# Order of a group's matmuls on high and low parts, and the last two of a pair moved behind the next pair's first tile

## The chip, the cores and the metric

The kernel runs on one core of one Trainium2 chip. The metric is the device time of one execution in microseconds (us): 1093.27 us as the median of three runs before the change (1089.42 to 1093.37). Rows come from one profiled execution, in which a hardware profiler recorded every instruction. The core has five engines that run their own queues and meet at semaphores: TensorE (PE, matmuls; PEld is its weight load), VectorE (DVE), ScalarE (ACT), GpSimd (POOL) and SyncE (SP). DMAs are issued here from SP's and POOL's queues.

## What is computed

Channel attention over a sequence of 6016 positions and 256 channels, and two MLPs behind it (6016 x 256, hidden width 2048). In short:

```python
s = kn.transpose(0, 2, 1) @ qn / tau        # q, k normalised over the sequence: 256 x 256 scores
a = softmax(s)
x = v @ a                                   # 6016 x 256
h = x @ moe_w_in;  y = (s * relu(h)**2 + b) @ moe_w_out
h = y @ moe2_w_in; out = (max(h, 0) + alpha * min(h, 0)) @ moe2_w_out
```

## The kernel before, in words

**High and low parts.** A matmul operand in fp32r keeps fewer bits than fp32. So each fp32 operand is split: the high part is a cast of the value (by ACT, or by DVE where the planner chooses so), the low part is the value minus its high part (always on DVE, line 714 for the activations). A product is three matmuls into one PSUM bank: high data with high weights, high data with low weights, low data with high weights (`s` = 0, 1, 2 in the code).

**Stages.** The scores and the softmax take the first 60 us or so. The attention itself is folded into the first MLP's input weights (`w1_mm`, line 624), which are made in four quarters during the first pairs. Then the two MLPs run one after the other, each over six chunks of the sequence. A chunk is two blocks of 512 positions (480 in the first and the last chunk), which are the columns of the matmuls, and goes through eight *pairs*; a pair is 256 of the 2048 hidden units. There are 96 pairs, `c` = 0 to 95, eight to a chunk: pairs 0 to 47 are the first MLP, 48 to 95 the second. Pairs whose `c` is a multiple of 8 begin a chunk.

**A pair, first layer** (`a_tile`, lines 658 to 688). Four tiles: two halves of the hidden units for each of two blocks of positions. A tile is six matmuls (lines 671, 672, 674) into the one bank `h`. ACT evacuates it with the activation (lines 682 and 686), the first two tiles into `gA[c % 2]`, of which there are two copies, the last two into slots 1 and 2 of `gB`, of which there is one.

**A pair, between the layers** (`g_ops`, lines 690 to 727). The second layer is a Strassen-Winograd product, seven products in place of eight. Its seven operands are formed from the four evacuated tiles: in the second MLP by four operations at line 705 (the leaky slope), in both by four sums and differences (lines 721, 722, 724, 725). They lie in four buffers, each with a high and a low half: `G[0]` (two operands), `G[1]` (one), `G[2]` (two), `G[3]` (two). `G[3]` is made last. The cast for the high half is at line 713 (shown as line 364 where ACT does it), the low half is line 714. Each buffer exists once.

**A pair, second layer** (`b_mms`, lines 729 to 752). 21 matmuls (line 743), three for each of the products P1 to P7, each product with a PSUM bank of its own that adds up over the eight pairs of a chunk. With the bank `h` all eight banks are taken. The products and their buffers, in the order of the list: P1, P2 on `G[0]`; P3 on `G[1]`; P5, P7 on `G[2]`; P6, P4 on `G[3]`. The weights `W["wB", p]` are split in the same way.

**After a chunk** (`results`, lines 754 to 836): the banks are copied by ACT (line 364, `cb<-P`), combined by seven additions on DVE (line 774), and in the second MLP transposed on DVE (line 824) and stored; in the first MLP they get bias and scale, are split and written to memory for the second.

**What sets the order.** All this is put into a list of operations with what they read and write (class `Plan`). TensorE's operations keep the order of the list. For ACT, DVE and the DMA issues (line `sp`, in fact POOL's and SP's queues) a planner goes through an estimated time: it takes the ready operation with the earliest due time, which comes from the place of its readers in TensorE's order, and an operation that overwrites a buffer waits for the buffer's readers. Operations with no near reader (results, preparation of the second MLP's weights) are taken where nothing more urgent is ready.

TensorE's order is written out in the loop at line 890. In turn `c` the four tiles of pair `c` are emitted, and the 21 matmuls of pair `c - 1` are spread behind them (5, 5, 5 and 6):

```python
for i, u in enumerate(users):
    u()
    upto = len(bs) * (i + 1) // len(users)
    while nb < upto:
        g, r, w, us = bs[nb]
        op("pe", us, g, r, w)
        nb += 1
```

So 45 matmuls stand between one pair's start and the next one's. `g_ops(c)` and, where a chunk ends, `results` follow. From `c` = 40 to 48 the loop also emits the loads of the second MLP's weights: `wB` (line 931) and `wA` (line 935), both issued on POOL's queue, as are the loads of `x` (line 858).

Of the kernel before, what the change touches and what calls it, by code (L numbers as in the profile page):

```python
# [43 lines left out]
def est(kind, n):  # L44
    return FIXED[kind] + n * COLUMN.get(kind, 0.00085)


class Plan:
# [7 lines left out]
    def op(self, eng, us, fn, reads=(), writes=(), due=None, late=0.0, boost=0.0, after=0.0, leave=BACKLOG[0]):  # L56
        o = dict(
            i=len(self.ops), eng=(eng,) if isinstance(eng, str) else eng, us=us, fn=fn,
            pre=set(), post=[], due=due, late=late, boost=boost, after=after, leave=leave,
            left=0, end=None,  # L60
        )
        for r in reads:
            if r in self.writer:
                o["pre"].add(self.writer[r])
        for w in writes:
            if w in self.writer:
                o["pre"].add(self.writer[w])
            o["pre"].update(self.readers.get(w, ()))
        for r in reads:
            self.readers.setdefault(r, []).append(o["i"])  # L70
        for w in writes:
            self.writer[w], self.readers[w] = o["i"], []
        o["pre"].discard(o["i"])
        self.ops.append(o)
        return o
# [103 lines left out]
def tile_channel_attention_mlp_mlp(  # L179
# [56 lines left out]
    def bank(tag, name):  # L236
        return ps.tile([P, CH], F32, tag=tag, name=name)
# [124 lines left out]
    def copy(eng, o, i):  # L362
        if eng == "act":
            nc.scalar.copy(o, i)  # L364
        else:
            nc.vector.tensor_copy(o, i)
# [41 lines left out]
    with tc.manual_schedule():  # L408
# [196 lines left out]
        op = pl.op  # L605
# [3 lines left out]
        def add_unit(n, after=0.0):  # L609
            if n >= NLATE + NRAW:  # L610
                op("sp", 0.6, lambda: load_w(n), [("R",)] if n < NEARLY else [],
                   [("raw", raw_slot(n)), ("low", raw_slot(n))], late=4.0)
            parts = units.get(n) or unit_parts(n)
            for p in parts[started.get(n, 0) :]:
                op(*p[:5], late=p[5] if len(p) > 5 else 0.0, after=after)
# [74 lines left out]
        def g_ops(c):  # L690
            ph, j, p = c // 48, c // 8 % NCHUNK, c % 8
            n = sizes[j]
            a = gA[c % 2]
            k11, k21, kt, k12, k22 = ("gA", c % 2, 0), ("gA", c % 2, 1), ("gB", 0), ("gB", 1), ("gB", 2)
            V = nc.vector
            B11, B21, T1, B12, B22 = a[:, 0, :n], a[:, 1, :n], *(gB[:, i, :n] for i in range(3))
            if ph == 0:
                op("act", est("square", 2 * n), lambda: nc.scalar.activation(
                    a[:, :, :n], a[:, :, :n], AF.Square), [], [k11, k21])
                for g, kk in ((B12, k12), (B22, k22)):  # L700
                    op("act", est("square", n), lambda g=g: nc.scalar.activation(g, g, AF.Square), [], [kk])  # L701
            else:
                for f2, g, kk in ((0, B11, k11), (1, B21, k21), (0, B12, k12), (1, B22, k22)):
                    al = al_sb[:, 2 * p + f2 : 2 * p + f2 + 1]
                    op("dve", est("stt", n), lambda g=g, al=al: V.scalar_tensor_tensor(  # L705
                        g, g, al, g, op0=ALU.mult, op1=ALU.max), [], [kk])

            def hilo(k, src, keys):
                m = len(keys)
                hi, lo = (G[k][:, y, :m, :n] if m > 1 else G[k][:, y, 0, :n] for y in (0, 1))  # L710
                kh = [("Gh", k, x) for x in range(m)]
                kl = [("Gl", k, x) for x in range(m)]
                op(either, HI(m * n), lambda e: copy(e, hi, src), keys, kh, leave=BACKLOG[ph])
                op("dve", est("tt", m * n), lambda: V.tensor_tensor(  # L714
                    lo, src, hi.bitcast(F32), ALU.subtract), keys + kh, kl)

            tt = est("tt", n)
            hilo(0, a[:, :, :n], [k11, k21])  # L720
            op("dve", tt, lambda: V.tensor_tensor(T1, B12, B11, ALU.subtract), [k11, k12], [kt])  # L721
            op("dve", tt, lambda: V.tensor_tensor(B12, B22, B12, ALU.subtract), [k22], [k12])  # L722
            hilo(1, B22, [k22])
            op("dve", tt, lambda: V.tensor_tensor(B11, B12, B11, ALU.add), [k12], [k11])  # L724
            op("dve", tt, lambda: V.tensor_tensor(B21, B21, B11, ALU.subtract), [k11], [k21])  # L725
            hilo(2, gB[:, 0:2, :n], [kt, k12])
            hilo(3, a[:, :, :n], [k11, k21])

        def b_mms(c):

            j, p = c // 8 % NCHUNK, c % 8
            n = sizes[j]
            first, last = p == 0, p == NPAIR - 1
            res = []
            for tag, (wb, k, x) in PROD.items():
                m = n + 2 if c < 8 and tag in ("P1", "P2", "P5") else n
                for s in range(3):
                    def go(tag=tag, wb=wb, k=k, x=x, s=s, m=m):
                        if first and s == 0:
                            acc_t[tag] = bank(tag, f"{tag}_{c}")  # L740
                        w = W["wB", p]
                        cols = m if s < 2 else n
                        nc.tensor.matmul(  # L743
                            acc_t[tag][:, :cols], w[:, int(s == 1), wb, :],
                            G[k][:, int(s == 2), x, :cols],
                            start=(first and s == 0), stop=(last and s == 2),
                        )

                    half = 1 if wb >= 3 else 0
                    kw = ("wBl" if s == 1 else "wBh", p) + ((1,) if half else ())  # L750
                    res.append((go, [kw, ("Gl" if s == 2 else "Gh", k, x)], [("bank", tag)], 0.0133 + n * 0.2134 / CH))
            return res
# [133 lines left out]
        for h in range(NC2):  # L886
            w1_out(0, h, f"P{h + 1}")
        NCYC = 2 * NCHUNK * NPAIR
        W1_AT = {1: (1, ("P6", "P4")), 3: (2, ("h", "h")), 5: (3, ("h", "h"))}
        for c in range(NCYC + 1):  # L890
            if c % 8 == 0 and 0 < c < NCYC:
                for x in range(2):
                    x_ops(c // 8, x)
            users = []
            if c < NCYC:
                users = [lambda i=i: a_tile(c, i) for i in range(4)]
            if c in W1_AT:
                qq, tags = W1_AT[c]
                for h in range(NC2):
                    def make(h=h):  # L900
                        w1_mm(qq, h, tags[h])
                        w1_out(qq, h, tags[h])
                    users.insert(2 + h, make)
            bs = b_mms(c - 1) if c else []
            nb = 0
            for i, u in enumerate(users):
                u()
                upto = len(bs) * (i + 1) // len(users)
                while nb < upto:
                    g, r, w, us = bs[nb]  # L910
                    op("pe", us, g, r, w)
                    nb += 1
            while nb < len(bs):
                g, r, w, us = bs[nb]
                op("pe", us, g, r, w)
                nb += 1
            if c < NCYC:
                g_ops(c)
            if c % 8 == 0 and c:
                results(c // 8 - 1)  # L920
            if c == 5:
                op("no", 0.0, switch, [], [("R",), ("R2",)])
                for n in (14, 15):
                    add_unit(n)
            if c == 8:
                for n in range(16, len(order)):
                    add_unit(n, after=(n - 16) * 19.0 + 100.0)
            if 40 <= c <= 48:
                p = c - 41
                if p >= 0:  # L930
                    op("sp", 0.7, lambda p=p: nc.gpsimd.dma_start(W["wB", p], W["wod"][p]),
                       [("wod", p)], [(x, p, *y) for x in ("wBh", "wBl") for y in ((), (1,))], late=6.0)
                if c < 48 and c % 2:
                    qq = (c - 40) // 2
                    op("sp", 0.7, lambda qq=qq: nc.gpsimd.dma_start(W["wA", qq], W["wid"][qq]),
                       [("wid", 2 * qq), ("wid", 2 * qq + 1)],
                       [(x, qq, h) for x in ("wAh", "wAl") for h in range(2)], late=6.0)
# [38 lines left out]
```

## Time and profile before

| | before |
|---|---|
| median of three runs | 1093.27 us (1089.42 to 1093.37) |
| the profiled execution | 1093.81 us |
| its span, first to last instruction | 1092.0 us |
| mean granted TensorE clock | 0.988 of full speed |
| matmuls (PE), busy | 1054.1 us |
| weight loads (PEld), busy | 857.1 us |
| DVE, busy | 1005.5 us |
| ACT, busy | 807.5 us |
| POOL, busy | 40.3 us |
| line 743, second layer, 2016 matmuls | 525.8 us busy, 10.4 us idle before them |
| lines 671, 672, 674, first layer, 2304 matmuls | 835.2 us busy (301.3 + 298.3 + 235.6), 5.3 us idle before them |

How to read it. An engine's busy time is the union of its instructions. A matmul's row is longer than its distance from the next one, since matmuls overlap in the array, so a busy PE need not be at its peak. "Idle before" is the time an engine stood still before a group of instructions, and the name behind `<-` is what ended the idle time. A row of a timeline merges neighbouring instructions of the same kind (`x6`).

### The profile page before, as it was taken

The numbers are of one execution on the slowest core, as the hardware profiler recorded it, in microseconds if no ns is written. First come the engines' busy times: TensorE is split into PE (matmuls) and PEld (weight loads), VectorE is DVE, ScalarE is ACT, GpSimd is POOL, SyncE is SP. The second block draws the span as 40 slices with busy tenths as digits, with TensorE's granted clock in tenths as the row PEclk, the third lists the DMA queues.
The fourth block names the chain that finished last, engine by engine and source line by source line (L and its number), as shares of the span: only waits on it lengthen the run. The fifth ranks groups of instructions, "written<-read, shape, count | busy, mean of one in ns | idle before, by whom it ended". The sixth has DMA issues, their size and how long they took to land.

```text
span 1092.0 us, 13134 instructions
## 1 busy us (share of the span) xinstructions
PE 1054.1 (97%) x4610; PEld 857.1 (78%) x4610; DVE 1005.5 (92%) x1451; ACT 807.5 (74%) x1171; POOL 40.3 (4%) x70
## 2 busy tenths in 40 slices
PE   8979999999999999999999999999999999999994
PEld 7847687888787877888888888787787787788783
DVE  3889999999999999988769999999999999999996
ACT  5569989999899889988877666566566567567563
POOL 0000000100100100000110100000000000000000
PEclk9979999999999999999999999999999999999998
DMA  9862013532433342122644211102102203102102
GB/s 352 270 137 77 20 36 54 138 126 57 146 114 57 111 131 58 58 88 60 232 150 171 73 38 49 27 19 69 30 1 87 30 1 85 30 1 47 29 1 37
DMA packets 129475, 90.00 MB, mean 82 GB/s; under 512 B 103808, under 2 KB 112768, under 8 KB 127872
## 3 DMA queue, kind: packets, MB, share of 16 engines
q1 hardware_dynamic: 113696, 39.35, 15.1%
q0 software_dynamic: 14848, 47.71, 13.5%
q10 hardware_dynamic: 864, 2.10, 0.6%
q8 instruction: 36, 0.59, 0.2%
q14 instruction: 31, 0.25, 0.1%
HBM read 59.12 MB, written 30.02 MB: 82 GB/s over the span
## 4 chain that ended last, share of the span: by engine, by line
PE 65%; DVE 15%; issue 9%; DMA 5%; ACT 4%; SPq 1%; DVEq 0%; POOL 0%; POOLq 0%; ACTq 0%
PE P L743 29%; PE h L671 12%; PE h L672 11%; PE h L674 11%; DVE G L714 6%; DMA qk<-in_q_dram 3%; DVE gA L705 1%; DVE cb L774 1%; SPq L403 1%; DVE gA L724 1%; DVE gB L705 1%; DVE gA L725 1%; PE wp L624 1%; DMA qk<-in_k_dram 1%; ACT G L364 1%
## 5 line engine op out<-in xcount | busy, mean ns | idle before, releaser
L743 PE MATMUL P<-G,wB 128*128 128x512 f32 (+2 forms) x2016 | 525.8, 389 | 10.4 <-DVE G L714 9.9
L743 PEld LDWEIGHTS P<-G,wB 128*128 128x128 f32 x2016 | 376.1, 188 | 97.2 <-DVE G L714 22.6
L671 PE MATMUL h<-x,wA 128*128 128x512 f32 (+1 forms) x768 | 301.3, 392 | 4.9 <-ACT gA L682 2.9
L672 PE MATMUL h<-x,wA 128*128 128x512 f32 (+1 forms) x768 | 298.3, 388 | 0.4 <-DVE wA L638 0.4
L714 DVE TENSOR_TENSOR G<-gA,G 128x1024 fp32r<-128x1024 f32 (+1 forms) x192 | 226.3, 1195 | 32.2 <-ACT G L364 30.9
L674 PE MATMUL h<-x,wA 128*128 128x512 f32 (+1 forms) x768 | 235.6, 388 | 0.0
L364 ACT CAST G<-gB 128x512 fp32r<-128x512 f32 (+1 forms) x192 | 156.7, 819 | 57.3 <-DVE gB L705 53.5
L364 ACT CAST G<-gA 128x1024 fp32r<-128x1024 f32 (+1 forms) x184 | 186.0, 1026 | 7.9 <-DVE gA L725 7.7
L671 PEld LDWEIGHTS h<-x,wA 128*128 128x128 f32 x768 | 144.9, 189 | 49.9 <-ACT gA L682 5.9
L714 DVE TENSOR_TENSOR G<-gB,G 128x512 fp32r<-128x512 f32 (+1 forms) x192 | 179.8, 937 | 4.5 <-ACT G L364 3.8
L674 PEld LDWEIGHTS h<-x,wA 128*128 128x128 f32 x768 | 145.3, 189 | 28.2
L672 PEld LDWEIGHTS h<-x,wA 128*128 128x128 f32 x768 | 145.3, 189 | 23.8 <-DVE wA L638 0.9
L686 ACT ACTIVATE gB<-h,sg_sb 128x512 f32<-128x512 f32 (+1 forms) x96 | 65.3, 680 | 66.4 <-PE h L674 66.3
L686 ACT ACTIVATE gA<-h,sg_sb 128x512 f32<-128x512 f32 (+1 forms) x96 | 65.3, 680 | 49.6 <-PE h L674 49.5
L682 ACT ACTIVATE gA<-h 128x512 f32<-128x512 f32 (+1 forms) x96 | 56.4, 588 | 32.6 <-PE h L674 29.8
L705 DVE SCALAR_TENSOR_TENSOR gB<-gB,al_sb 128x512 f32<-128x512 f32 (+1 forms) x96 | 70.6, 736 | 5.5 <-ACT gB L686 5.5
L682 ACT ACTIVATE gB<-h 128x512 f32<-128x512 f32 (+1 forms) x96 | 56.4, 588 | 20.4 <-PE h L674 20.0
L705 DVE SCALAR_TENSOR_TENSOR gA<-gA,al_sb 128x512 f32<-128x512 f32 (+1 forms) x96 | 70.7, 737 | 0.7 <-ACT gA L686 0.2
L722 DVE TENSOR_TENSOR gB<-gB 128x512 f32<-128x512 f32 (+1 forms) x96 | 64.7, 674 | 5.4 <-ACT gB L701 4.0
L721 DVE TENSOR_TENSOR gB<-gB,gA 128x512 f32<-128x512 f32 (+1 forms) x96 | 64.8, 675 | 1.7 <-ACT gB L701 1.2
L725 DVE TENSOR_TENSOR gA<-gA 128x512 f32<-128x512 f32 (+1 forms) x96 | 64.7, 674 | 0.3
L724 DVE TENSOR_TENSOR gA<-gB,gA 128x512 f32<-128x512 f32 (+1 forms) x96 | 64.6, 673 | 0.0
(119 smaller groups left out, 740.7 us busy)
## 6 DMA issues: line engine op xcount, KB each, us to landing
yd<-yo POOLq DMA_DIRECT2D x16, 512.0 KB, 3.0
x<-yd POOLq DMA_DIRECT2D x8, 1024.0 KB, 5.1
wod<-stage POOLq DMA_DIRECT2D x8, 896.0 KB, 4.0
wB<-wod POOLq DMA_DIRECT2D x8, 896.0 KB, 5.8
raw<-in_moe_w_in_dram SPq DMA_DIRECT2D x12, 512.0 KB, 4.3
raw<-in_moe_w_out_dram SPq DMA_DIRECT2D x12, 512.0 KB, 3.6
qk<-in_q_dram SPq DMA_DIRECT2D x7, 640.0 KB, 11.1
vraw<-in_v_dram SPq DMA_DIRECT2D x64, 64.0 KB, 2.5
```

Source lines behind the costliest of these rows:

```text
L364: nc.scalar.copy(o, i)
L671: nc.tensor.matmul(t[:, :n], w[:, h, 0, fs], xx[:, h, 0, :n], start=(h == 0), stop=False)
L672: nc.tensor.matmul(t[:, :n], w[:, h, 1, fs], xx[:, h, 0, :n], start=False, stop=False)
L674: nc.tensor.matmul(t[:, :n], w[:, h, 0, fs], xx[:, h, 1, :n], start=False, stop=(h == NC2 - 1))
L682: op("act", est("relu", n), lambda: nc.scalar.activation(g, hb.pop((c, i))[:, :n], AF.Relu), [("bank", "h")], [kg], boost=60.0)
L686: op("act", est("scaled", n), lambda: nc.scalar.activation(g, hb.pop((c, i))[:, :n], AF.Copy, scale=sg_sb[:, fc : fc + 1]), [("bank", "h") ...
L705: op("dve", est("stt", n), lambda g=g, al=al: V.scalar_tensor_tensor(g, g, al, g, op0=ALU.mult, op1=ALU.max), [], [kk])
L714: op("dve", est("tt", m * n), lambda: V.tensor_tensor(lo, src, hi.bitcast(F32), ALU.subtract), keys + kh, kl)
L721: op("dve", tt, lambda: V.tensor_tensor(T1, B12, B11, ALU.subtract), [k11, k12], [kt])
L724: op("dve", tt, lambda: V.tensor_tensor(B11, B12, B11, ALU.add), [k12], [k11])
L725: op("dve", tt, lambda: V.tensor_tensor(B21, B21, B11, ALU.subtract), [k11], [k21])
L743: nc.tensor.matmul(acc_t[tag][:, :cols], w[:, int(s == 1), wb, :], G[k][:, int(s == 2), x, :cols], start=(first and s == 0), stop=(last an ...
```

## The change

In `b_mms` the list is grouped by buffer. Within a group the matmuls on the high part come first (`s` = 0 and 1 of each product), then those on the low part (`s` = 2). For `G[0]` that is P1 0, P1 1, P2 0, P2 1, P1 2, P2 2, and so on.

In the loop the last two of a pair's list (P6 and P4 on the low part of `G[3]`) are held over in `over` and are emitted behind the first tile of the next turn, except where a chunk ends, where all are emitted. `g_ops(c - 1)` is now emitted behind that first tile and the held-over matmuls, as it overwrites `G[3]`. Behind the four tiles stand 5, 5, 5 and 6 second-layer matmuls as before, of which the first two are the held-over ones; 4, 5, 5 and 5 where nothing was held over (`c % 8 == 1`); 5, 6, 6 and 6 where `c % 8 == 0`. The loads of `wB` are emitted one turn later.

```diff
--- before.py
+++ after.py
@@ -728,13 +728,18 @@
 
         def b_mms(c):
 
+
             j, p = c // 8 % NCHUNK, c % 8
             n = sizes[j]
             first, last = p == 0, p == NPAIR - 1
             res = []
+            groups = {}
             for tag, (wb, k, x) in PROD.items():
-                m = n + 2 if c < 8 and tag in ("P1", "P2", "P5") else n
-                for s in range(3):
+                groups.setdefault(k, []).append((tag, wb, x))
+            for k, tags in groups.items():
+                for s, (tag, wb, x) in [(s, t) for ss in ((0, 1), (2,)) for t in tags for s in ss]:
+                    m = n + 2 if c < 8 and tag in ("P1", "P2", "P5") else n
+
                     def go(tag=tag, wb=wb, k=k, x=x, s=s, m=m):
                         if first and s == 0:
                             acc_t[tag] = bank(tag, f"{tag}_{c}")
@@ -886,6 +891,14 @@
         for h in range(NC2):
             w1_out(0, h, f"P{h + 1}")
         NCYC = 2 * NCHUNK * NPAIR
+        def b_ops(bs, nb, upto):
+            while nb < upto:
+                g, r, w, us = bs[nb]
+                op("pe", us, g, r, w)
+                nb += 1
+            return nb
+
+        over = []
         W1_AT = {1: (1, ("P6", "P4")), 3: (2, ("h", "h")), 5: (3, ("h", "h"))}
         for c in range(NCYC + 1):
             if c % 8 == 0 and 0 < c < NCYC:
@@ -901,21 +914,21 @@
                         w1_mm(qq, h, tags[h])
                         w1_out(qq, h, tags[h])
                     users.insert(2 + h, make)
-            bs = b_mms(c - 1) if c else []
-            nb = 0
+            bs = over + (b_mms(c - 1) if c else [])
+            nb, before = 0, len(over)
+            over = bs[len(bs) - 2 :] if c % 8 else []
+            bs = bs[: len(bs) - len(over)]
             for i, u in enumerate(users):
                 u()
+                if i == 0 and c:
+                    nb = b_ops(bs, 0, before)
+                    g_ops(c - 1)
                 upto = len(bs) * (i + 1) // len(users)
-                while nb < upto:
-                    g, r, w, us = bs[nb]
-                    op("pe", us, g, r, w)
-                    nb += 1
-            while nb < len(bs):
-                g, r, w, us = bs[nb]
-                op("pe", us, g, r, w)
-                nb += 1
-            if c < NCYC:
-                g_ops(c)
+                nb = b_ops(bs, nb, upto)
+            if c == NCYC:
+                nb = b_ops(bs, 0, before)
+                g_ops(c - 1)
+            nb = b_ops(bs, nb, len(bs))
             if c % 8 == 0 and c:
                 results(c // 8 - 1)
             if c == 5:
@@ -925,8 +938,8 @@
             if c == 8:
                 for n in range(16, len(order)):
                     add_unit(n, after=(n - 16) * 19.0 + 100.0)
-            if 40 <= c <= 48:
-                p = c - 41
+            if 40 <= c <= 49:
+                p = c - 42
                 if p >= 0:
                     op("sp", 0.7, lambda p=p: nc.gpsimd.dma_start(W["wB", p], W["wod"][p]),
                        [("wod", p)], [(x, p, *y) for x in ("wBh", "wBl") for y in ((), (1,))], late=6.0)
```

## Rows read from the trace of the kernel before

**Rows 1.** The page, part 1: busy time, share of the span, instructions.

```profile
span 1092.0 us, 13134 instructions
...
PE 1054.1 (97%) x4610; PEld 857.1 (78%) x4610; DVE 1005.5 (92%) x1451; ACT 807.5 (74%) x1171; POOL 40.3 (4%) x70
```

**Rows 2.** Windows: us; busy time and instructions by engine; PEclk, DMA share, GB/s.

```profile
163.70:497.95 334.25, 330.26 (x1441) 269.08 (x1440) 320.21 (x487) 302.03 (x464) 21.66 (x33) 1.00 0.34 93
497.95:576.16 78.21, 78.21 (x361) 67.51 (x360) 59.34 (x77) 65.48 (x98) 8.51 (x16) 1.00 0.50 163
576.16:1062.35 486.19, 480.17 (x2116) 391.25 (x2115) 469.82 (x632) 309.72 (x421) 9.41 (x16) 1.00 0.17 43
```

**Rows 3.** Timeline of PE, 512 columns: start us, us, engine, line, operation.

```profile
477.55 0.39 PE L671 MATMUL h<-x,wA 128*128 128x512 f32 x1
...
478.91 1.30 PE L743 MATMUL P<-G,wB 128*128 128x512 f32 x5
...
486.39 1.52 PE L743 MATMUL P<-G,wB 128*128 128x512 f32 x6
487.75 0.39 PE L671 MATMUL h<-x,wA 128*128 128x512 f32 x1
```

**Rows 4.** Timeline of PE, two pairs of 480 columns.

```profile
517.66 0.38 PE L671 MATMUL h<-x,wA 128*128 128x480 f32 x1
...
527.41 0.38 PE L671 MATMUL h<-x,wA 128*128 128x480 f32 x1
```

**Rows 5.** Timeline of PE at the end of a loaded pair.

```profile
759.13 0.61 PE L743 MATMUL P<-G,wB 128*128 128x512 f32 x2
760.09 1.21 PE L743 MATMUL P<-G,wB 128*128 128x512 f32 x4 [0.34 <-DVE G L714]
761.14 0.40 PE L671 MATMUL h<-x,wA 128*128 128x512 f32 x1
```

**Rows 6.** Line 714: who waited for it (us, times).

```profile
  PEld P L743: 20.6, 28
  PE P L743: 8.9, 23
```

**Rows 7.** PE's waits from 163.7 to 1066: us in total, times, longest us.

```profile
PE h L671 <- ACT gA L682: 0.8, 2, 0.6
```

**Rows 8.** Windows: one chunk of the second MLP, and one of its pairs.

```profile
740.02:823.89 83.87, 82.85 (x361) 66.72 (x360) 81.12 (x108) 53.12 (x71) 1.06 (x2) 1.00 0.16 38
...
803.44:813.67 10.23, 10.23 (x46) 8.34 (x45) 9.72 (x13) 6.20 (x8) 0.00 (x0) 1.00 0.00 1
```

**Rows 9.** Timeline of DVE, three loaded pairs.

```profile
754.21 1.22 DVE L714 TENSOR_TENSOR G<-gB,G 128x1024 fp32r<-128x1024 f32 x1
...
758.22 0.69 DVE L774 TENSOR_TENSOR cb<-cb,cb 128x512 f32<-128x512 f32 x1
758.82 2.35 DVE L714 TENSOR_TENSOR G<-gA,G 128x1024 fp32r<-128x1024 f32 x2
...
761.75 0.68 DVE L721 TENSOR_TENSOR gB<-gB,gA 128x512 f32<-128x512 f32 x1
...
772.66 0.68 DVE L721 TENSOR_TENSOR gB<-gB,gA 128x512 f32<-128x512 f32 x1
...
776.33 1.22 DVE L714 TENSOR_TENSOR G<-gB,G 128x1024 fp32r<-128x1024 f32 x1
```

**Rows 10.** Timeline of ACT in the same pairs.

```profile
751.88 0.69 ACT L686 ACTIVATE gA<-h,sg_sb 128x512 f32<-128x512 f32 x1 [0.32 <-PE h L674]
...
756.83 0.69 ACT L686 ACTIVATE gB<-h,sg_sb 128x512 f32<-128x512 f32 x1 [1.82 <-PE h L674]
757.41 1.99 ACT L364 CAST G<-gA 128x1024 fp32r<-128x1024 f32 x2
...
778.64 0.69 ACT L686 ACTIVATE gB<-h,sg_sb 128x512 f32<-128x512 f32 x1 [1.82 <-PE h L674]
```

**Rows 11.** The page, part 6: DMA issues, KB each, us to landing.

```profile
wB<-wod POOLq DMA_DIRECT2D x8, 896.0 KB, 5.8
```

## The prediction, made before the changed kernel was run

> **What bounds the kernel now.** First the page's engine shares [rows 1]: the matmuls cover 97% of the span and VectorE (DVE) 92%. Both look full, and neither share says which one sets the pace, so I read the pace itself. In a stretch without a stall [rows 3] the six matmuls of the tile that starts at 477.55 take until 478.91, that is 1.36 us or 0.227 each, and the six second-layer matmuls from 486.39 to 487.75 take the same. So the distance from one matmul to the next doesn't depend on which bank, weight or part it uses, and a reordered list costs nothing by itself. A pair (45 matmuls) takes 487.75 - 477.55 = 10.20 us; with 480 columns 527.41 - 517.66 = 9.75 us [rows 4]. That is TensorE's floor.
>
> Pairs 8 to 94 lie between 163.70 and 1062.35. 64 of them have 512 columns and 23 have 480, so their floor is 64 x 10.20 + 23 x 9.75 = 877.1 us. The three windows [rows 2] add up to 898.65 us: 21.6 us over the floor. They are 7.9 over in the first (32 pairs), 0.2 in the second, where DVE is busy for 59.3 of 78.2 us, and 13.5 in the third (47 pairs). This 21.6 us is all that a better order can win in the steady part; the start before 163.7 us isn't touched by it (part 4).
>
> Next, where it is lost. Waits of second-layer matmuls (line 743) for line 714 on DVE, which makes the low parts of G: 28 weight loads waited and 23 matmuls left TensorE idle, for 8.9 us [rows 6]. One of them in full [rows 5]: after tile 3 two matmuls start at 759.13 (high G, both weights of P6); the third, P6 on the low part of G3, should start 2 x 0.227 later at 759.58 and starts at 760.09. The last four then take 1.05 instead of 0.91 us. So the stall costs 0.51 + 0.14 = 0.65 us, though the idle column shows only 0.34: about 0.31 a stall on top. All waits: 8.9 + 28 x 0.31 = 17.6 us. From the other side: 21.6, less 0.03 of scatter a pair (a stall-free one takes 10.23, rows 8) x 87 = 2.6, less two waits for ScalarE (ACT), 0.8 + 2 x 0.31 = 1.4 [rows 7], leaves 17.6. I use **17 us**. The timeline puts them all but one at the same matmul, P6 on G3's low part, about 27 times.
>
> Why it is late: ACT casts G3's high part only at 757.41, after the third tile's evacuation [rows 10]; DVE meanwhile begins an addition of the last chunk's results (758.22) and makes the low part from 758.82 on, in 1.22 us [rows 9]. It ends at 760.04, and the matmul starts at 760.09.
>
> **The change part by part.** Positions are counted in matmuls from the start of a pair's first tile: in the example the row at 759.13 is position 39, so that pair began 39 x 0.227 earlier, at 750.28. "Loaded" pairs are the three after a chunk's first, in which DVE also works off the last chunk's results.
>
> 1. *High parts first within a group.* The low-part matmuls of G0, G1, G2 move from positions 8, 20, 29 to 18, 28, 39; the high-part ones that lead a group move by 2 (part 2 takes two places). Nothing is added. Gain in itself about 0: no wait stands there now, except one on G0.
>
> 2. *P6 and P4 on G3's low part run behind the next pair's first tile.* P6's moves from position 41 to 45 + 6 = 51: ten matmuls, 2.27 us later. In the example it is due at 761.86 and its operand is ready at 760.04 plus a signal, so 1.8 us are spare. All 17 us of stalls are inside that slack if DVE stays where it is.
>
> 3. *What is late next.* If TensorE no longer stands still in three loaded pairs of a chunk, it runs ahead of DVE by 0.65 us more in each. G3's high part (cast from 757.41, two casts in 1.99, the first done by 758.4) is due at position 41, 759.59: 1.2 us spare. The tighter one is gB, which exists once: the third tile's evacuation into it must wait for the subtraction that makes G2's low part. In the first loaded pair this ends at 755.43 and the evacuation starts at 756.83 (1.40 spare); in the third it ends at 777.55 against 778.64 (1.09) [rows 9, 10]. By then TensorE would be 1.3 us earlier, so the evacuation is 0.2 us late. I give back 0.25 us for each of nine chunks: **+2 us**.
>
> 4. *Pairs whose number is 1 modulo 8* no longer start with a remainder but leave one: 19 matmuls over four tiles instead of 21, so four instead of five between first and second tile (0.91 instead of 1.13 us). The h bank is single, so the second tile waits for the first one's evacuation: in the example this lasts from 751.88 to 752.57 [rows 10], and with four matmuls the tile is due at 750.28 + 10 x 0.227 = 752.55. Between 0 and 0.23 us in 11 pairs; I take **+1 us**, as 0.02 plus a signal is near the low end. Start: the two tiles of pair 1 keep three matmuls behind each, 0.
>
> 5. *Emission of the G operations behind the next pair's first tile.* DVE and ACT follow the planner's due times, not the emission, and the first tile writes only gA's other copy: 0, covered by that copy. Looser due times for low parts may let the planner put other work ahead; that is the cover of part 3 and a rival below.
>
> 6. *wB's reloads one pair later* on POOL's queue (line 931), so that the reader of the last weights is past. Eight loads of 5.8 us [rows 11] move by 9.75 us and are used seven pairs (68 us) later; behind them in that queue stand reloads of wA and x with as much room: 0.
>
> 7. *Tail.* The last P4 no longer follows P6's three matmuls; P6, the first that the closing additions need, still starts when G3's low part is done: 0 to -0.5, taken as 0.
>
> Sum: -17 + 2 + 1 = -14 us. The profiled execution took 1093.8 us (span 1092.0 and 1.8 around it); the median of the runs shown is 1093.3. 1093.8 - 14 = 1079.8; against the median 1079.3. I say **1079.5**, for its own part between 1073.5 (17.6, the ACT waits and the tail won as well) and 1086.
>
> **The rivals.**
> *A, DVE becomes the bound.* For: in the chunk from 740.02 it is busy 81.1 of 83.9 us, and the floor is 81.6 [rows 8]. Against: busy time includes pauses between dependent operations. The loaded stretch from 761.75 to 772.66 has 12 operations for G and 3 for results (about 0.60 each by the starts 758.22 and 758.82, rows 9): 10.91 - 1.8 = 9.1 us a pair, 8 x 9.1 + 11 x 0.60 = 79.4 us a chunk, 2.2 under the floor. If the pauses stay, chunks of the second MLP win nothing, and those of the first, whose weight preparation can slip into the idle second window, win some 5.5: 1088.
> The Trainium skill (VectorE: DVE Perf Modes, The DRAIN you can't avoid) speaks for A: the next operation doesn't start until the pipeline has emptied, so lengths would add up; the trace disagrees, since an addition of 0.69 us has its successor 0.60 us after its start, and with 108 operations a chunk, 0.09 us each, the rule would make some 90 us of a chunk that took 83.9.
>
> *B, slower: gB's single copy.* The planner sees the low part of G2 due ten matmuls later and puts other operations first. From 1.85 us later than now (1.40 spare and some 0.45 until the h bank is wanted) the third tile's evacuation holds up the fourth in each pair. If all 2.27 us are spent: 0.4 us x 88 - 17 = +18, so 1112. Against: the planner knows this reader and derives a due time from it.
>
> *C, nothing happens:* the waits are put down to the wrong operand, or every order is late by one operation again because DVE fills what it is given: 1093. Against: the end at 760.04 and the start at 760.09 fit.
>
> **How the numbers follow.** Forecast 0.72, A 0.14, B 0.06, C 0.08. What a measurement of this kernel can tell from no change is about 0.5%, 5.5 us, so faster means under 1087.8. All but 0.01 of the forecast and half of A are faster: 0.78. Half of A, all of C and that 0.01 are within it, less 0.01 of C: 0.15. B and that 0.01: 0.07. The range leaves out B, C and little of the ends: 1073 to 1091.
>
> **What would show it.** Right: line 743 has at most a third of its waits for line 714; the chunk that took 83.87 takes 81.7 to 82.3; DVE idle in it falls from 2.75 to below 1.2; P6's low matmul stands behind a first tile without a gap. Part 3 would show as line 671 waiting for ACT in the third loaded pair, part 4 in the pairs numbered 1 modulo 8. Wrong, by A: DVE without idle time and the same number of waits, moved to other matmuls; by B: ACT's evacuation of gB waiting for line 714 in most pairs; by C: the same waits at the moved matmul.

## The result, and the profile after

| | before | after |
|---|---|---|
| median | 1093.08 us (7 runs, 1089.29 to 1093.37) | 1084.45 us (7 runs, 1079.08 to 1086.66) |
| the profiled execution | 1093.81 us, span 1092.0 | 1086.66 us, span 1084.9 |
| pairs 8 to 47 | 412.46 us | 408.52 us |
| pairs 48 to 94 | 486.19 us | 481.80 us |
| pair 95 to the end | 29.7 us | 30.5 us |

The ratio of the medians is 0.9916, with a 95% interval of 0.9895 to 0.9937: faster by 8.6 us, where 14 were forecast. Executions of one and the same program come out up to 8 us apart, most of it from what happens before pair 8 (last section), so besides the ratios the text compares the steady stretch, pairs 8 to 94: 898.65 us before, 890.32 after, floor 877.1. The 21.6 us that lay over the floor have become 13.2. The stretch is read from one profiled execution of each kernel. Two executions of one program differed in it by 1.4 us (e10 below), so a smaller difference than that is not told apart here.

Line numbers move with the edit: 743 of before is 748 after, 774 is 779, 824 is 829. The lines of `a_tile` and `g_ops` stay.

The page, part 1, of the changed kernel, answering to [rows 1]:

```profile
PE 1053.2 (97%) x4610; PEld 860.5 (79%) x4610; DVE 1005.1 (93%) x1461; ACT 799.7 (74%) x1161; POOL 39.4 (4%) x70
```

As before, the shares tell nothing: they are the same work in a slightly shorter span. The windows do. Pairs 8 to 47, pairs 48 to 94, and the chunk that answers to the first of [rows 8]:

```profile
164.01:572.53 408.52, 406.47 (x1802) 336.89 (x1800) 382.19 (x573) 360.03 (x552) 29.30 (x49) 1.00 0.37 107
572.53:1054.33 481.80, 478.87 (x2116) 392.87 (x2115) 466.60 (x630) 310.54 (x422) 9.43 (x16) 1.00 0.17 43
...
734.98:818.25 83.27, 82.72 (x362) 66.91 (x361) 81.01 (x108) 53.29 (x71) 1.06 (x2) 1.00 0.16 39
```

The chunk went from 83.87 to 83.27 us, not to the 81.7 to 82.3 forecast; DVE still idles 83.27 - 81.01 = 2.26 us in it, where below 1.2 was expected. So the chunk had something else that held it. What did go is the old wait. Who waited for line 714 in pairs 8 to 94, against [rows 6]:

```profile
  PEld P L748: 0.7, 1
  PE P L748: 0.3, 1
```

28 waits of weight loads have become one, 8.9 us of idle matmul time 0.3. The list of PE's waits in the same stretch, against [rows 7], shows the successor:

```profile
PE h L671 <- ACT gB L686: 2.6, 5, 0.7
PE h L671 <- ACT gA L682: 0.8, 1, 0.8
PE h L671 <- ACT gB L682: 0.8, 1, 0.8
PE P L748 <- DVE G L714: 0.3, 1, 0.3
PE P L748 <- ACT G L364: 0.2, 1, 0.2
```

First-layer matmuls (line 671) now wait for ACT's evacuation of the bank `h` into `gB`, five times by up to 0.7 us. Pairs 65 to 67 in PE's timeline of the changed kernel show all of it: the old stall gone, and two new ones.

```profile
747.01 1.07 PE L748 MATMUL P<-G,wB 128*128 128x512 f32 x4
748.01 0.50 PE L671 MATMUL h<-x,wA 128*128 128x512 f32 x1
...
766.01 0.39 PE L671 MATMUL h<-x,wA 128*128 128x512 f32 x1
...
767.37 1.30 PE L748 MATMUL P<-G,wB 128*128 128x512 f32 x5
768.51 0.39 PE L671 MATMUL h<-x,wA 128*128 128x512 f32 x1
...
772.43 1.29 PE L748 MATMUL P<-G,wB 128*128 128x512 f32 x5
774.27 0.50 PE L671 MATMUL h<-x,wA 128*128 128x512 f32 x1 [0.55 <-ACT gB L686]
```

- **The moved matmuls.** P6 and P4 on G3's low part are the first two of the five at 767.37, behind the first tile of pair 67. The five take until 768.51, that is 1.14 us or 5 x 0.227: no gap.
- **The fourth tile of pair 67.** The five at 772.43 end their turn at 772.43 + 1.14 = 773.57. The tile starts at 774.27, 0.71 late, and its second matmul follows at 774.61, 0.34 behind instead of 0.23: 0.82 us.
- **The second tile of pair 65** (a pair numbered 1 modulo 8). Due at 747.01 + 4 x 0.227 = 747.92, it starts at 748.01, and its second matmul is again 0.11 late: 0.20 us.

DVE and ACT around pair 67 say why the fourth tile is late. First DVE, then ACT, of the changed kernel:

```profile
764.35 2.32 DVE L714 TENSOR_TENSOR G<-gA,G 128x1024 fp32r<-128x1024 f32 x2
...
768.45 0.68 DVE L722 TENSOR_TENSOR gB<-gB 128x512 f32<-128x512 f32 x1
769.05 0.69 DVE L714 TENSOR_TENSOR G<-gB,G 128x512 fp32r<-128x512 f32 x1
...
772.18 1.22 DVE L714 TENSOR_TENSOR G<-gB,G 128x1024 fp32r<-128x1024 f32 x1
```

```profile
770.10 0.69 ACT L686 ACTIVATE gA<-h,sg_sb 128x512 f32<-128x512 f32 x1 [1.33 <-PE h L674]
770.69 1.04 ACT L364 CAST G<-gB 128x1024 fp32r<-128x1024 f32 x1
771.63 2.00 ACT L364 CAST G<-gA 128x1024 fp32r<-128x1024 f32 x2
773.54 0.67 ACT L686 ACTIVATE gB<-h,sg_sb 128x512 f32<-128x512 f32 x1
```

Read from the end: the third tile's evacuation into `gB` (773.54) waits for the subtraction that reads `gB` for G2's low part (772.18 to 773.40). That needs G2's cast, which ran only at 770.69. Its operand was ready at 768.45 + 0.68 = 769.13, and ACT idled for 1.33 us before 770.10. The planner holds a ready operation back when one of the evacuations on the same engine would be ready more than `LOOK` = 0.15 us before it ended. A cast of 1.04 us started at 769.13 ends at 770.2; the evacuation was ready at 770.1. In the trace that is 0.1 us too long, close to the limit. The planner works with its own estimates, which no trace shows; by them it must have been over the limit, as e5 below confirms. So the cast was put behind the evacuation, 1.5 us later, and everything on the single `gB` behind it.

Over pairs 8 to 94, from the distances of matmul starts: 26 of the 27 stalls of P6 are gone, and so is the one on G0's low part in pair 50, together 15.8 us with their restarts. The 27th stands in pair 8. Against that stand the fourth tile in eight pairs of the second MLP (50, 52, 61, 67, 75, 83, 90, 92), 5.1 us; the second tile in the pairs numbered 1 modulo 8, 1.5 us; one wait of about 1.0 each in pairs 31 and 43. Some 1.3 us in pair 8 (1.4 before) and 3.1 of scatter (2.6 before) stood there in much the same size.

### The profile page after: what moved, and what is told of

Its sections match the earlier page's. It is cut to its first block, busy times and chain, and to the rows that moved or that the text cites. A ratio compares the mean times of both kernels' runs of the same rounds, so it can differ in the third digit from the quotient of the medians.

```text
span 1084.9 us, 13135 instructions
## 1 busy us (share of the span) xinstructions
PE 1053.2 (97%) x4610; PEld 860.5 (79%) x4610; DVE 1005.1 (93%) x1461; ACT 799.7 (74%) x1161; POOL 39.4 (4%) x70
## 4 chain that ended last, share of the span: by engine, by line
PE 56%; DVE 2%; ACT 2%; DMA 1%; issue 1%; DVEq 0%; POOL 0%; ACTq 0%; POOLq 0%
PE P L748 26%; PE h L671 10%; PE h L672 10%; PE h L674 10%; DVE G L714 1%; ACT G L364 1%; DMA yd<-yo 1%; ACT gB L686 1%; DMA wid<-stage 1%; DVE cb L779 0%; ACT gA L686 0%; DVE gB L722 0%; DVE gB L705 0%; DVE gA L705 0%; DVE gA L724 0%
## 5 line engine op out<-in xcount | busy, mean ns | idle before, releaser
L748 PE MATMUL P<-G,wB 128*128 128x512 f32 (+2 forms) x2016 | 518.4, 388 | 1.3 <-DVE G L714 0.6
L364 ACT CAST G<-gA 128x1024 fp32r<-128x1024 f32 (+1 forms) x175 | 177.2, 1026 | 7.9 <-DVE gA L725 7.4
```

The costliest lines, as they stand in the source:

```text
L748: nc.tensor.matmul(acc_t[tag][:, :cols], w[:, int(s == 1), wb, :], G[k][:, int(s == 2), x, :cols], start=(first and s == 0), stop=(last an ...
```

## The experiments

"Stretch" is pairs 8 to 94 of each kernel's profiled execution, its two parts pairs 8 to 47 and 48 to 94. Ratios are to the kernel before.

| kernel | median us | ratio, 95% interval | 8 to 47 | 48 to 94 | stretch |
|---|---|---|---|---|---|
| before | 1093.08 | | 412.46 | 486.19 | 898.65 |
| the change | 1084.45 | 0.9916 (0.9895 to 0.9937) | 408.52 | 481.80 | 890.32 |
| e1 order alone | 1080.48 | 0.9896 (0.9871 to 0.9921) | 407.84 | 478.82 | 886.66 |
| e8 order of G3 alone | 1079.24 | 0.9879 (0.9843 to 0.9915) | 407.17 | 479.57 | 886.74 |
| e2 hold-over, order of G3 | 1083.98 | 0.9921 (0.9891 to 0.9951) | 408.62 | 480.71 | 889.33 |
| e3 change, second `gB` | 1075.39 | 0.9858 (0.9816 to 0.9900) | 408.37 | 476.19 | 884.56 |
| e6 order, second `gB` | 1082.81 | 0.9908 (0.9877 to 0.9939) | 407.93 | 479.53 | 887.46 |
| e7 before, second `gB` | 1089.25 | 0.9986 (0.9964 to 1.0009) | 412.30 | 487.21 | 899.51 |
| e4 other spread | 1084.37 | 0.9932 (0.9906 to 0.9958) | 410.25 | 480.73 | 890.98 |
| e5 LOOK 0.35 | 1085.77 | 0.9953 (0.9929 to 0.9977) | 413.29 | 478.30 | 891.59 |
| e10 wB later (runs as the change) | 1078.53 (one execution) | | 408.08 | 480.86 | 888.94 |
| e11 LOOK 0.35, wB later (runs as e5) | 1085.73 | 0.9936 (0.9919 to 0.9953) | 412.96 | 477.46 | 890.42 |
| e9 hold-over late, second `gB` | 1074.52 | 0.9861 (0.9845 to 0.9878) | 407.86 | 476.11 | 883.97 |

**Which half of the change earns the gain? e1: the order alone, nothing held over.**

```diff
-            over = bs[len(bs) - 2 :] if c % 8 else []
+            over = []
```

> Part 1 of the change alone: the list is grouped by buffer with high parts first, but nothing is held over behind the next pair's first tile. P6 on G3's low part then stands at position 43 instead of 41, 0.45 us later. Theory (slack against DVE's lag): a stall of before was some 0.5 us late in each of three loaded pairs, and without it DVE falls behind further, so 0.45 us of slack are used up in the first loaded pair and the waits come back in the second and third; 0.4 to 0.5 us are won per chunk, 4 to 6 us in all, 1087 to 1089, and line 748 still has 15 to 25 waits for line 714. Rival (the order alone is the gain, the hold-over is not needed): the waits shrink to a handful and the time is that of the change, 1082 to 1086.

The stretch came to 886.66 us, 3.7 under the change: the rival was right on the time, and the time lies even below its range (1080.48 against 1082 to 1086). On the waits the theory was right. Who waited for line 714 in e1, pairs 8 to 94:

```profile
  PEld P L748: 8.6, 22
  ACT gA L682: 0.7, 1
  PE P L748: 0.7, 2
```

22 weight loads still wait, but the matmuls behind them idle for 0.7 us in all. DVE of e1 has the reason in numbers:

```profile
760.60 2.36 DVE L714 TENSOR_TENSOR G<-gA,G 128x1024 fp32r<-128x1024 f32 x2
```

The first of the two operations is the low part of G3 that P6 reads in pair 66. It ends at 761.82. By PE's timeline pair 66 of e1 starts at 752.17. At the old place, position 41, P6 would be due at 752.17 + 41 x 0.227 = 761.5 and be 0.3 late; at position 43 it is due at 761.9 and loses nothing. In pair 66 of the change the same operation (the first of the two at 764.35 above) ends near 765.5, and the held-over matmul ran at 767.37, with 1.9 to spare. Two places were enough.

My theory against it, that without the hold-over the lateness would build up from pair to pair, fell: in the loaded pairs 65, 66 and 67 of e1 the low part of G3 ends 9.79, 9.65 and 9.60 us into the pair (before: 9.78, 9.81 and 9.80).

**e8: only G3's group reordered, nothing held over.** This separates the two places won on G3 from the rest of the reordering.

```diff
-                for s, (tag, wb, x) in [(s, t) for ss in ((0, 1), (2,)) for t in tags for s in ss]:
+                for s, (tag, wb, x) in (
+                    [(s, t) for ss in ((0, 1), (2,)) for t in tags for s in ss] if k == 3
+                    else [(s, t) for t in tags for s in range(3)]
+                ):
...
-            over = bs[len(bs) - 2 :] if c % 8 else []
+            over = []
```

> Only G3's group has its high parts first, nothing is held over, G0 to G2 keep the order of before. P6 on G3's low part stands at position 43 instead of 41. Theory (these two places are the whole effect of part 1, since no low part but G3's is late): the same as the order-only kernel, 886.7 us within 1.5 for pairs 8 to 95, about 1080.5. Rival (the later due times of the other low parts matter, because they leave DVE free for G3): 3 to 8 us slower than the order-only kernel, with more than ten waits for line 714.

886.74 us against 886.66 of e1: without the hold-over the reordering of G0 to G2 is worth nothing that can be told, and P6's move from position 41 to 43 is the whole gain, 11.9 of the 21.6 us.

**e2: the hold-over as in the change, but G0 to G2 in the old order** (the first half of e8's diff alone).

> The hold-over of P6's and P4's matmuls on G3's low part alone: only G3's group has its high parts first, the groups of G0, G1 and G2 keep the old order. Theory (only G3's low part was ever late): same time as the change within 2 us, 1082.5 to 1086.5, and hardly a wait of line 748 for line 714. Rival (the room won on G0 to G2 is needed too, since DVE now runs behind TensorE): 3 to 8 us slower than the change, with new waits of matmuls on G0's or G2's low part.

889.33 us, 1.0 under the change, which is within the scatter. So the order of G0 to G2 isn't what makes the change dearer than e1; the hold-over is. The waits did not stay away as expected, though: in pairs 50, 60, 67, 75 and 83 the first matmul on G2's low part is 0.34 to 0.41 us late, and the fourth tile behind it 0.25 to 0.36. In pair 67 the cause is the late cast again (769.78, behind the evacuation at 769.20): the low part follows it at 771.32, and the matmul starts at 772.60. In the change the matmuls on G2's low part stand eight places further back, so the late cast shows only at the fourth tile. With the hold-over DVE's and ACT's operations for G fall later in the pair: in pair 67 of the change the operand of G2's cast (line 722) starts 768.45 - 766.01 = 2.44 us into the pair, in e1 2.29. In e1 the cast just fits ahead of the evacuation. ACT of e1 in its pair 67:

```profile
765.45 1.06 ACT L364 CAST G<-gB 128x1024 fp32r<-128x1024 f32 x1 [0.21 <-DVE gB L722]
766.55 0.69 ACT L686 ACTIVATE gA<-h,sg_sb 128x512 f32<-128x512 f32 x1
```

By these rows 0.15 us of DVE time decide whether the cast runs at once or 1.5 us later: a cliff, not a slope. e5 below tests it.

**Is it the single `gB`? e3: the change, with a second copy of the two slots of `gB` that G2 reads, for odd pairs of the second MLP.** The copy lies in a buffer of the weight preparation that is idle by then.

```diff
+        gB2 = raw_t[2].rearrange("p a c t -> p a (c t)").bitcast(F32)
+        two = lambda c: c >= 48 and c % 2 == 1
...
-            g = gA[c % 2][:, f2, :n] if x == 0 else gB[:, 1 + f2, :n]
+            g = gA[c % 2][:, f2, :n] if x == 0 else gB2[:, 1, :n] if two(c) and not f2 else gB[:, 1 + f2, :n]
...
-            hilo(2, gB[:, 0:2, :n], [kt, k12])
+            hilo(2, (gB2 if two(c) else gB)[:, 0:2, :n], [kt, k12])
```

> The change, and in the second MLP a second copy of gB's slots 0 and 1 for pairs of odd number, in the space of a weight buffer that is idle by then, so that the third tile's evacuation no longer waits for the reader of the last pair's G2 operand. Theory (gB's single copy is what the change runs into): the eight waits of a fourth tile for ACT's evacuation of the third in the second MLP (5.1 us with their restarts in the changed kernel's trace) are gone or below 1.5 us, and the time falls by 4 to 5.5 us, to 1079 to 1081. Rival (DVE is the bound, gB only the place where it shows): the waits turn up at P6's high or low part or at another tile, and the time stays within 1.5 us of the change.

Pairs 48 to 94 of e3:

```profile
566.80:1042.99 476.19, 476.19 (x2117) 393.79 (x2116) 466.33 (x630) 311.37 (x423) 9.40 (x16) 1.00 0.18 44
```

481.80 became 476.19, 5.6 us less where the late fourth tiles had cost 5.1, and in this stretch the list of PE's waits is empty. PE is busy throughout, and DVE for 466.33 of 476.19 us: at 98% busy it holds up nobody, so rival A isn't the bound of this kernel. The low part of G3 ends 7.2 to 7.9 us into the loaded pairs 57 to 83 here; before the change it ended at 9.7 to 9.8, in the change at 7.6 to 9.8. The median fell by 9 us, more than the 4 to 5.5 expected; the stretch accounts for 5.8 of it.

**e6 and e7: is the second copy worth something by itself?** The same edit on e1 (order alone) and on the kernel before.

> Part 1 alone (high parts first within a group, no hold-over) with the second copy of gB's slots in the second MLP. Theory (in the order-only kernel gB is never the limit; its loss is the 0.3 us waits for G3's low part, which a second copy doesn't touch, and the hold-over pays only where gB doesn't bind): the stretch from pair 48 to 95 stays at 478.8 us within 1, so 2 to 3 us above the 476.2 us of hold-over and second copy together. Rival (the second copy helps by itself): it falls to 476 to 477, and the hold-over has no use at all.

> The kernel before with the second copy of gB's slots in the second MLP, nothing else. Theory (before the change the bound was P6 on G3's low part, and gB had 1.1 us to spare): the waits of line 743 for line 714 stay and the stretch from pair 48 to 95 stays at 486.2 us within 1; time within 1.5 us of before. Rival (gB held back DVE or ACT even then): 1.5 to 6 us faster than before.

No, in both: pairs 48 to 94 took 479.53 (e1: 478.82) and 487.21 (before: 486.19), and e7's interval holds 1. The copy pays only where the hold-over has pushed the work against it, and the hold-over only with the copy: of the four combinations with high parts first, 478.8 (neither), 479.5 (copy), 481.8 (hold-over), 476.2 (both).

**Is it the order on ACT? e5: the planner's limit from 0.15 to 0.35 us**, so that G2's cast may go ahead of the evacuation.

```diff
-LOOK = 0.15
+LOOK = 0.35
```

> The change, with the planner allowed to start a cast on ACT that would delay a tile's evacuation by up to 0.35 us instead of 0.15 (one constant, LOOK). Theory (a cliff in ACT's order: in the third loaded pair of the changed kernel G2's operand is ready about 0.2 us too late for its cast to fit in ahead of the second tile's evacuation, the cast is put behind it, 1.5 us later, and with it the low part that gB's next evacuation waits for): the fourth tile's waits of 0.8 to 0.95 us in pairs 61, 67, 75 and 83 are gone, the stretch from pair 48 to 95 falls from 481.8 us by 3 to 5 us, and the time by 2 to 5 us. Rival (DVE's lag alone is the cause, ACT's order doesn't matter): the waits stay, or as much is lost in tiles that start late by 0.1 to 0.2 us everywhere; within 1.5 us of 481.8.

ACT of e5 in the same pair 67:

```profile
771.81 1.06 ACT L364 CAST G<-gB 128x1024 fp32r<-128x1024 f32 x1 [0.98 <-DVE gB L722]
772.77 0.68 ACT L686 ACTIVATE gA<-h,sg_sb 128x512 f32<-128x512 f32 x1
```

The cast stands ahead of the evacuation, though its operand came no earlier (3.29 us into the pair, in the change 3.12). The long waits of the fourth tile are gone, and pairs 48 to 94 take 478.30, 3.5 us less: the cliff is shown. The whole gained nothing, though: 1085.77 us, where 2 to 5 less than the change were expected. The same limit rules the first MLP as well, and there pairs 8 to 47 went from 408.52 to 413.29. PE of e5 in pair 43:

```profile
527.75 0.48 PE L671 MATMUL h<-x,wA 128*128 128x480 f32 x1 [2.92 <-ACT gA L682]
...
529.66 2.20 PE L748 MATMUL P<-G,wB 128*128 128x480 f32 x5
531.66 0.52 PE L671 MATMUL h<-x,wA 128*128 128x480 f32 x1
```

One wait of 2.9 us, and after it five matmuls took 531.66 - 529.66 = 2.00 us, 0.40 each instead of 0.217, at a granted clock of 0.81 over 525 to 534. Pair 43 lies 4.8 us over its floor, in the change 1.0. Behind the wait stands a cast of ACT into `yo`, which waits for a store to memory (`yd<-yo`) to land, in e5 for 3.73 us, in the change for 1.30 (at 522.52).

**e4: another spread**, six matmuls behind the first tile of the pairs numbered 1 modulo 8, against part 4's small wait.

```diff
-                upto = len(bs) * (i + 1) // len(users)
+                upto = -(-len(bs) * (i + 1) // len(users)) if c % 8 == 1 and c > 8 else len(bs) * (i + 1) // len(users)
```

> The change, with the 19 matmuls of a pair numbered 1 modulo 8 spread as 5, 5, 5 and 4 behind the four tiles instead of 4, 5, 5 and 5 (pairs 9 to 89). Theory (part 4 of the prediction: with four matmuls the first tile's evacuation isn't covered): the late second tiles of these pairs, 1.5 to 2 us over eleven of them in the changed kernel's trace, are gone, and the time falls by 1 to 2 us, to 1082.5 to 1083.5; these pairs then last 9.75 us with 512 columns instead of up to 10.05. Rival (the fourth tile's evacuation needs the fifth matmul as much, since the next pair's first tile follows it): the late tile moves to the next pair's first one and the time stays.

890.98 us against 890.32: no gain. The wait left the second tile and came back as up to 0.16 us at the first tile of the next pair; pair 23 gained a wait of 1.2. This spread doesn't win those 1.5 us; no other was tried.

**e10 and e11: pair 43.** One of its stores lands late (after 6.8 us, median 3.6, among the four from 505 to 532) behind a load of `wA` and one of `wB` that POOL issues just ahead of it. Both kernels are meant to load `wB` one pair later, e10 on the change, e11 on e5.

```diff
-            if 40 <= c <= 49:
-                p = c - 42
+            if 40 <= c <= 50:
+                p = c - 43
```

> The change, with the loads of wB for the second MLP one more pair later (two later than before the change). Theory (in the changed kernel the first of these loads and a load of wA stand right in front of the stores of the first MLP's results on POOL's queue and share the DMA engines with them, and ACT's cast into the store buffer waits in pair 43): the wait of pair 43's first tile for ACT, 1.0 us with its restart, is gone, and pairs 8 to 48 take 407.3 to 407.8 instead of 408.5 us. Rival (that wait comes from ACT's or DVE's order, not from the queue): it stays at 0.7 to 1 us.

> The wider window for casts (0.35 us) and the later loads of wB together, on the change. Theory (the wider window was right about the fourth tiles and lost its gain only to a wait of 2.9 us in pair 43 behind the store of results, after which the clock fell): pairs 48 to 95 stay at 478.3 within 0.5, the 2.9 us wait is gone, pairs 8 to 48 take 409 to 410.5 us instead of 413.3, and the time is 3 to 5 us under that of the wider window alone. Rival (the store's wait belongs to the wider window): it stays, and so does the time.

The wB load and the store behind it on POOL, in the change and then in e10 (`wA` is issued 2.8 us ahead in both):

```profile
515.19 0.53 POOL L944 DMA_DIRECT2D wB<-wod  x1 [2.28 <-DVE yo L820]
515.71 0.54 POOL L823 DMA_DIRECT2D yd<-yo  x1
```

```profile
508.05 0.53 POOL L944 DMA_DIRECT2D wB<-wod  x1 [2.29 <-DVE yo L820]
508.57 0.54 POOL L823 DMA_DIRECT2D yd<-yo  x1
```

The rows are the same, to 0.01 us in their distance (0.52). The planner orders the loads by their readers, so the place of emission moved nothing: in the traces every engine of e10 runs the same instructions in the same order as in the change, and every engine of e11 as in e5. The wait stayed, 0.7 us in e10 and 2.3 in e11, and e11's time is that of e5. So neither run tests the loads. They are second executions of the change and of e5, and show the scatter: stretches of 888.94 against 890.32 and of 890.42 against 891.59.

That the two loads delay the store is therefore not shown. For it speaks that the store issued right behind them is the slowest of four in three traces: 7.4 us before (at 519.91), 6.8 in the change, 7.0 in e1 (at 514.78), where the others take 2.9 to 4.9. A late store alone does not make the wait, since before and in e1 no tile of pair 43 waits. What else it takes stays open.

**e9: what the runs point to.** High parts first everywhere, the hold-over only in the second MLP, with the second `gB` (e3's edit, and):

```diff
-            over = bs[len(bs) - 2 :] if c % 8 else []
+            over = bs[len(bs) - 2 :] if c % 8 and c > 48 else []
```

> High parts first in both MLPs, the hold-over only in the second MLP (pairs from 49 on), and there the second copy of gB's slots. Theory (the hold-over pays only where gB has two copies): pairs 8 to 48 take as long as in the order-only kernel, 407.2 to 407.9 us, pairs 48 to 95 as in the kernel with hold-over and second copy, 476.2 within 0.7, together 883 to 884.5; 5 to 8 us less than the changed kernel in the median, 1076 to 1079. Rival (each gain is paid back where the two orders meet, or the planner makes another order of it): 886 or more for pairs 8 to 95, and no more than 4 us under the change.

Pairs 48 to 94 of e9:

```profile
565.16:1041.27 476.11, 476.11 (x2115) 393.44 (x2113) 466.53 (x631) 310.39 (x422) 9.40 (x16) 1.00 0.18 43
```

883.97 us is the shortest stretch of all, 6.35 under the change and 6.9 over the floor, of which some 3 are scatter. Both parts came out as expected; the median, 1074.52 us, is below the expected 1076 to 1079. The ratio of 0.9861 (0.9845 to 0.9878) doesn't touch the change's interval. Against e3 the stretch differs by only 0.6 us, which their ratios can't tell apart.

## Why the prediction was right, and where it was wrong

**What bounds the kernel: right.** TensorE's floor with 0.65 us a stall at P6 on G3's low part explained the time; with the matmul moved, 26 of P6's 27 stalls went and the one on G0, worth 15.8 us with their restarts against the 17 taken. Most of the rest stands in pair 8, whose waits (1.4 us, about half of them for a weight) stayed.

**Part 1, "gain in itself about 0": wrong.** It counted position 51 as what removes the stall and gave the order nothing. e8 shows the two places from 41 to 43 worth 11.9 us of stretch. I had the lateness (0.51 us) and the two places (0.45 us) side by side and didn't subtract them.

**Part 2: right in mechanism, wrong in worth.** The slack is there (1.9 us in pair 66), but the stalls it removes were already down to some 0.22 us each in 20 places after part 1, and the price of the hold-over was higher than that: 890.32 with it, 886.66 without. So the prediction is right for the two parts together and wrong on their shares: it gave all 17 us to the hold-over and nothing to the two places, which alone win 12. That the time lies in the range is no evidence for this split.

**Part 3, +2 us: right place, wrong size.** This is the term that missed by most. The fourth tile, held up through `gB`'s single copy, is what came next, as named. But I took it as lag that grows by 1.3 us and overruns 1.09 of slack, 0.25 a chunk, and mostly in the third loaded pair. It was 0.82 us in pairs 67, 75 and 83, 0.93 in pair 61 and 0.38 to 0.55 in four others, 5.1 in all, because ACT's cast of G2 changed places with an evacuation and came 1.5 us later at one stroke (shown in pair 67; with e5's limit all but one of the eight waits went). e3 removed the copy's limit and 5.6 us with it. Rival B is this mechanism in nearly every pair; it appeared in eight.

**Part 4, +1: held.** 0.06 to 0.22 us in each of the eleven pairs, 1.5 in all, inside 0 to 2.5.

**Parts 5 and 6, 0: partly wrong.** Emission order indeed doesn't matter (e10), but the order that the planner derives did move in the first MLP: waits of 1.0 us each in pairs 31 and 43, the latter behind a store.

**Part 7, 0: wrong by 0.85.** The tail runs 30.5 instead of 29.7 us. The last low part of G3 ends 16.3 us after pair 95 starts, before 15.4 and in e1, without the hold-over, 15.6. DVE is later in its pair with the hold-over.

**The sum.** -15.8 for the stalls, -1.7 for the second-tile waits that stood there before (most of them in [rows 7]), +5.1, +1.5, +2.1 and +0.6 of scatter: -8.2 in the stretch, which measured -8.3. With +0.3 at the start and +0.85 in the tail the span fell by 7.1 (1092.0 to 1084.9); the medians by 8.6.

**Rivals.** A fell with e3. The rule set beside it, that the next operation starts only when the pipeline has emptied (the Trainium skill, VectorE: DVE Perf Modes, The DRAIN you can't avoid), is not what this trace shows either: the 0.68 us operation at 768.45 has its successor at 769.05, after 0.60. The same section of the Trainium skill adds, which the prediction left out, that an operation that isn't held starts earlier. C fell with the waits for line 714.

## What to carry to other kernels

When an operand is late by about half a microsecond, subtract that from what each reordering gives before reaching for the larger one: two positions took 12 us of the loss here, and the eight more cost 3.7 us until the next single buffer had a second copy. A planner that starts long operations only if they fit ahead of an urgent one answers to small shifts in jumps, so look in the timeline at which operations stand within 0.2 us of changing places. And test a removed wait together with the buffer behind it: neither the copy nor the hold-over paid alone, both did together.

## What was unexpected in the hardware

Executions differ by 4 to 5 us in pairs 0 to 7, though the work there is the same: 99.35 us in the change and 94.72 in e10, the same program, and 99.47 before and 94.73 in e7, whose edit touches only the second MLP. (Up to 2 us more come from ahead of pair 0: the change reaches it at 64.66, e10 at 62.54.) PE in the first tiles of pair 0, in the profiled execution of before and then of e3, each with the window up to pair 8:

```profile
72.70 0.60 PE L671 MATMUL h<-x,wA 128*128 128x480 f32 x1
73.10 0.60 PE L672 MATMUL h<-x,wA 128*128 128x480 f32 x1
...
64.23:163.70 99.47, 93.80 (x365) 70.34 (x364) 93.88 (x172) 85.98 (x141) 0.00 (x0) 0.93 0.21 58
```

```profile
70.82 0.38 PE L674 MATMUL h<-x,wA 128*128 128x480 f32 x1
71.04 0.38 PE L673 MATMUL h<-x,wA 128*128 128x480 f32 x1
...
63.69:158.43 94.74, 88.58 (x363) 66.46 (x362) 93.52 (x174) 84.76 (x139) 0.00 (x0) 1.00 0.23 63
```

Matmuls of 480 columns are 0.40 us apart in the one and 0.22 in the other, as at the lower (1.2 GHz) and the upper (2.4 GHz) of the two clock levels; the granted clock is 0.93 of full speed over the one window and 1.00 over the other, and the windows differ by 4.7 us. In before the tile ahead of these had waited 1.45 us for ACT, in e3 1.25, in e7 1.26. The same fall follows the 2.9 us wait in pair 43 of e5. Why near-equal gaps lower the clock in one execution and not in the other wasn't settled. It is why the kernels here are compared by their steady stretch as well as by medians.
